# Five small moves of work around the turn of a fused linear-attention and gated-MLP forward and backward kernel: key sums, stores of r, loads of x, the r sums of tile 6, a fill between squares

## The chip, the core and the metric

The kernel runs on one core of a Trainium2 chip. All times are microseconds of device time of that core (us); one execution is one run of the whole program. Six runs of the kernel before took 828.26 to 830.65, median 829.41.

## What is computed

The reference is one transformer block and its gradients. With `x` of 2048 rows and 640 columns in bf16, 32 heads of 20 columns each, and `g` the gradient of the output:

```python
pq, pk = phi(q), phi(k)                    # phi(t) = where(t > 0, t + 1, exp(t)) + 1e-6
kv  = einsum("bhsd,bhse->bhde", pk, v)
z   = einsum("bhsd->bhd", pk)              # the key sums
den = einsum("bhqd,bhd->bhq", pq, z)[..., None] + 1e-6
o   = einsum("bhqd,bhde->bhqe", pq, kv) / den
h   = x + o.reshape(B, S, D) @ wo          # q, k, v = layernorm(x) @ wqkv
out = h + (silu(n @ w1) * (n @ w3)) @ w2   # n = layernorm(h)
```

The outputs are `out` and the gradients of `x`, `wqkv`, `wo`, `w1`, `w3`, `w2`.

## The kernel before

The 2048 rows are 16 tiles (`ST`) of 128 rows, in four groups (`SC`) of four; 640 columns are five blocks (`DT`) of 128. The order of the work on every engine is written out by hand: an engine executes its instructions in the order in which the Python code issues them, and the framework adds the waits that data and reused buffers ask for. So is the order in the three DMA queues that matter here: SP's (`dma`, `dmaT`, the second a transposing DMA), GpSimd's (`dmaG`) and ScalarE's (`A.dma_start`). An instruction that waits at the head of an engine or a queue holds up all behind it.

**Phase 1** (lines 430 to 570) normalises x, makes keys, values and a part of the queries, and sums over the keys. `m_part` accumulates a key-by-x matrix for each column block, `z_late` the key sums of blocks 2 to 4. `z_row` (line 324) spreads the key sums over all partitions: it multiplies a matrix of ones by diagonal matrices `dz` (two for blocks 0 and 1, three for blocks 2 to 4) into PSUM, and ScalarE copies the result to `Zb`. It is called twice (lines 533, 534), on the two banks of one PSUM tile `bigx`. The queries then get their denominators: for tile t, `r_prod` multiplies pq by `Zb` on GpSimd into `pr`, `r_red` sums per head on VectorE, `r_inv` adds 1e-6 and inverts, `r_scale` scales pq to r in place, and `r_T` issues a transposing DMA of it into `pqT` on SP's queue. `r_head` is `r_red`, `r_inv`, `r_scale` and `r_T` in one.

**The turn** is the single call of `run` at lines 801 to 809, a list of steps. `q_late` makes the remaining queries (each two halves of five 320-column matmuls, line 260); `f2_wT(i)` makes a row block of the folded output matrix and transposes it by DMA into `Wp` (line 628), five DMAs in all; `f2_half(t, j)` (line 780, body from 578) makes half j of h for tile t: five matmuls of `pqT` with `Wp` (line 586) into a PSUM tile `at`, then either an addition of x on VectorE (line 591; it is so for the j = 0 halves of tiles 0 to 3 and for tile 4) or, with x added on TensorE by the identity (line 584), a copy on ScalarE (line 589), and then statistics on VectorE. The second half ends with mean and variance, and GpSimd raises the variance to the power -1/2 (`ln_rs`, line 154). `f2_hn(t)` normalises the row tile on VectorE (line 160) and stores it on SP's queue; `f2_ht(t)` transposes it on TensorE (tile `trh`, line 677) and ScalarE copies it to `pqT` (line 678). `mlp_ghh(n)` is five 512-column matmuls of a piece of the MLP's gradient, which depend on nothing that the turn makes; ScalarE copies the result. `r_store`, `r4_out`, `q_out`, `f2_m_out`, `f2_w_out` are stores on GpSimd's queue. `load_x` brings x back into `x_sb` on SP's queue.

Two pools of buffers matter. `pql`, with four buffers, holds pq, later r, of tiles 4 to 7 and afterwards of the tiles that `r_load` brings back. The tag `h2`, with two buffers, holds the products `pr` of even tiles, then `hn` of tiles 2 and 3.

**The MLP** (line 849 on) goes through four groups of 512 rows and 14 column blocks each. `mlp(c, fc)` issues ten 512-column matmuls (line 369; five, from w1, then five, from w3), and ScalarE reads their PSUM tiles four times: `sig`, `s2`, `gate` (lines 705 to 707) and `up` (line 713). The PSUM tag `mm` has four buffers; TensorE gets one back when ScalarE has read it. The buffers of `up` lie on memory that the turn used for `pr` of tile 7. For each two blocks VectorE computes seven products and sums (line 741), and GpSimd's queue stores two of them to `gg_d`; the buffers of `gate` are two, so that block pair k + 2 may be written only when pair k's store has landed.

**Behind the MLP** come the weight gradients of w2 (line 955), the gradient towards h (line 1000) and the attention's backward part. In the squares (lines 1252 to 1295) five blocks of `dwoT` and five of `gm` are made: `square` (six matmuls of 140 columns into a PSUM tile of tag `dkv`, three buffers), `unload` (ScalarE copies 380 columns, then VectorE 260, line 1236), and for `gm` a few transposes `trk` into another `dkv` buffer (line 1284) with a copy on VectorE (line 1285). `fill(1)` puts eight 320-column matmuls of an independent job (line 1198) between them. Five `tensor_scalar` of VectorE make `gzd` (line 1278).

Of the kernel before, what the change touches and what calls it, by code (L numbers as in the profile page):

```python
# [55 lines left out]
def kernel(  # L56
# [19 lines left out]
    V, A, T, G, SY = nc.vector, nc.scalar, nc.tensor, nc.gpsimd, nc.sync  # L76
# [51 lines left out]
    Zb = cp.tile([P, D], BF16, name="Zb")  # L128

    class Stats:  # L130
# [8 lines left out]
        def run(self, src, a, b):  # L139
            for t in range(a, b):  # L140
                for j in range(2):
                    self.part(src, t, j)
# [32 lines left out]
    pf = pool("pf", "right")  # L175
    p1 = pool("p1", "right")
    ps = pool("p1p", space=PSUM)
# [6 lines left out]
    def load_x(a, b):  # L184
        dma(out=x_sb[:, a:b, :], in_=xS[:, a:b, :])
# [77 lines left out]
    def p1_mm(t, n0):  # L263
        acc = ps.tile([P, 2, 512], F32, name="big", bufs=2)
        for j in range(2):
            p1_half(acc[:, j, 0:HD], t, n0 + j * HD)
        return acc
# [40 lines left out]
    dz = {}  # L308
# [12 lines left out]
        for m in ms:  # L321
            z_diag(m)

    def z_row(ms, acc):

        for i, m in enumerate(ms):
            T.matmul(acc[:, i * P:(i + 1) * P], lhsT=ones[:], rhs=dz[m][:], start=(i == 0), stop=True,
                     skip_group_check=True)
        A.copy(out=Zb[:, ms[0] * P:(ms[-1] + 1) * P], in_=acc[:, 0:len(ms) * P])

    pr = {}

# [145 lines left out]
    for t in range(ST):  # L478
        k = p1_mm(t, D)
# [49 lines left out]
        go()  # L529
    z_late((2, 3, 4), big())  # L530
    m_part(2, range(10))
    zr = ps.tile([P, 2, 512], F32, name="bigx", tag="big", bufs=2)
    z_row((0, 1), zr[:, 0])
    z_row((2, 3, 4), zr[:, 1])
    r_prod(0)
    q_tile(5)
    r_prod(1)
# [31 lines left out]
    m_part(4, range(11, ST))  # L569
    m_end(4)  # L570
    ps.release()
    load_x(0, 2)


    ps = pool("pap", space=PSUM)
    hn, hnT, hhT = {}, {}, {}
# [43 lines left out]
    def f2_wT(i):  # L620

        acc = [ps.tile([P, 512], F32, name="wt", tag=("o2", "at")[i % 2], bufs=2) for _ in range(2)]
        for c, a, b, bank, off, first in SQ:
            T.matmul(acc[bank][:, off:off + (b - a) * DH], lhsT=wo[:, c, i * P:(i + 1) * P],
                     rhs=bd[:, c, a * DH:b * DH], start=first, stop=True, skip_group_check=True)
        for bank, (a, b) in enumerate(((0, SPLIT_D), (SPLIT_D, H))):
            (A.copy, V.tensor_copy)[bank](out=pkx[0][:, i, a * DH:b * DH], in_=acc[bank][:, 0:(b - a) * DH])
        dmaT(out=Wp[:, :, i * P:(i + 1) * P], in_=pkx[0][:, i, :])
# [30 lines left out]
        dma(out=pqs[t], in_=pq_v[:, t, :])  # L659

    def f2_hn(t):
        hn[t] = (pf.tile([P, D], BF16, name="hn", tag="h2", bufs=2) if 2 <= t < TPC else
                 pf.tile([P, D], BF16, name="hn", bufs=2))
        ln2.norm(hn[t][:], x_sb[:, t, :], t)
        dma(out=hn_v[:, t, :], in_=hn[t][:])
# [131 lines left out]
    def kv3():  # L797
        for m in (2, 3, 4):
            f2_kv(m)

    run((q_late, 10, f2_mT), (q_late, 11, kv3), (phi_rest,), (r_store, 4, 5),
        (q_late, 12, lambda: (f2_wT(0), f2_wT(1))), (q_late, 13, lambda: (f2_wT(2), f2_wT(3))), (phi_rest,),
        (q_late, 14, lambda: f2_wT(4)), (load_x, 2, 4), (r_head, 5), (r_prod, 7), (r_red, 6), (r_inv, 6), (f2_m_out,), (f2_w_out,),
        (load_x, 4, 8), (q_out, 10, 14), (r_store, 5, 6), (load_w2T, 8 * P, 10 * P), (mlp_ghh, 4), (q_late, 15),
        (sig_table,), (f2_half, 0, 0), (f2_half, 1, 0), (mlp_ghh, 5), (f2_half, 0, 1), (f2_half, 1, 1), (f2_hn, 0),
        (f2_half, 2, 0), (f2_hn, 1), (load_w2T, 10 * P, F), (f2_half, 2, 1),
        (f2_ht, 0), (f2_half, 3, 0), (f2_hn, 2), (f2_half, 3, 1), (mlp_ghh, 6), (f2_ht, 1), (mlp_ghh, 7), (f2_ht, 2),
        (f2_hn, 3), (f2_half, 4, 0), (f2_ht, 3), (f2_half, 4, 1), (r_scale, 6), (r_T, 6), (r_red, 7), (r_inv, 7),
        (r_scale, 7), (r_T, 7), (r4_out,), (r_store, 6, 8), (q_out, 8, 10))
    p1.release()  # L810
    pa = pool("pa", "right")

# [36 lines left out]
    for c in range(SC):  # L849
# [8 lines left out]
        for fc in range(FT):  # L858
# [22 lines left out]
            if c == SC - 1 and fc in (1, 2, 5, 6):  # L881
                i = (1, 2, 5, 6).index(fc)
# [29 lines left out]
    ps = pool("pcp", space=PSUM)  # L912
# [35 lines left out]
    for fc in range(FT - 1):  # L948
        b, i = divmod(fc, 4)
        if fc == FT - 2:  # L950
            gw2_tail()
        acc = ps.tile([P, 2, 512], F32, name="gw", bufs=4)
        for j in range(2):
            for t in range(ST):
                T.matmul(acc[:, j, 0:HD], lhsT=hb[b][:, t, i * P:(i + 1) * P], rhs=g2[:, t, j * HD:(j + 1) * HD],  # L955
                         start=(t == 0), stop=(t == ST - 1))
# [23 lines left out]
    ps = pool("pbp", space=PSUM)  # L980
# [3 lines left out]
    gz = cp.tile([P, DT], F32, name="gz")  # L984
# [234 lines left out]
    ps = pool("pdp", space=PSUM)  # L1219
# [14 lines left out]
    def unload(acc, out):  # L1234
        for bank, (a, b) in enumerate(((0, SPLIT_D), (SPLIT_D, H))):
            (A.copy, V.tensor_copy)[bank](out=out[:, a * DH:b * DH], in_=acc[:, bank, 0:(b - a) * DH])

    def fill(n):
        for _ in range(n):
            next(jobs, None)  # L1240
# [4 lines left out]
    for m, (a, b) in enumerate(M_H):  # L1245
        n = (b - a) * DH
        acc = ps.tile([P, 512], F32, name="gkvT", tag="dkv", bufs=3)
        for c in range(DT):
            T.matmul(acc[:, 0:n], lhsT=woT[:, c, m * P:(m + 1) * P], rhs=QT[:, c, a * DH:b * DH], start=(c == 0),
                     stop=(c == DT - 1))  # L1250
        masked(gkvT, acc[:, 0:n], m)
    dwoT = U1.tile([P, DT, D], BF16, name="dwoT", tag="W6")
    for i in range(DT):
        unload(square(qp, kvN, i), dwoT[:, i, :])
        if i > 0:
            fill(1)
    br.release()
    bo.release()
# [4 lines left out]
    gzd = small[:, 3 * DT, :].rearrange("p (m q) -> p m q", q=P)  # L1263
# [5 lines left out]
    def load_pk(c):  # L1269
        pkb[c] = dx.tile([P, 2, D], BF16, name="pkb", bufs=4)  # L1270
        (dma if c < 4 else dmaG)(out=pkb[c][:], in_=pk_v[:, c * 2:(c + 1) * 2, :])
# [2 lines left out]
    g_k = gqkv[1] = U1.tile([P, ST, D], BF16, name="g_k", tag="S0")  # L1274
    for n in range(4):
        load_pk(n)
    for m in range(DT):
        V.tensor_scalar(out=gzd[:, m, :], in0=ident[:], scalar1=gz[:, m:m + 1], scalar2=None, op0=ALU.mult)

    for i, (c, ms) in enumerate(SQ_BLOCKS):  # L1280
        unload(square(wqT[:, 2 * DT:, :], gkvT, i), gm[:, i, :])
        tr = ps.tile([P, len(ms), P], BF16, name="trk", tag="dkv", bufs=3)
        for k, m in enumerate(ms):
            T.transpose(tr[:, k, :], gkvT[:, m, c * P:(c + 1) * P], ident[:])
        V.tensor_copy(out=gkv_b[:, c, ms[0] * P:(ms[-1] + 1) * P].rearrange("p (i q) -> p i q", q=P), in_=tr[:])
        if i > 0:
            fill(1)
        dmaT(out=wqT[:, 2 * DT:, i * P:(i + 1) * P], in_=gm[:, i, :])
    acc = d_acc()
    for m in range(DT):  # L1290
        T.matmul(acc[:, m // 4, m % 4 * P:(m % 4 + 1) * P], lhsT=ones[:], rhs=gzd[:, m, :], start=(m % 4 == 0),
                 stop=True, skip_group_check=True)
# [3 lines left out]
    for t in range(ST):  # L1296
        c, i = divmod(t, TPC)
        u = t // 2
        acc = d_acc()
        for j in range(2):  # L1300
            for k in range(DT):
                T.matmul(acc[:, j, 0:HD], lhsT=xnT[c][:, k, i * P:(i + 1) * P], rhs=gm[:, k, j * HD:(j + 1) * HD],  # L1302
                         start=(k == 0), stop=(k == DT - 1))
# [7 lines left out]
        if t in (2, 5, 8, 11, 14):  # L1311
            n = t // 3
            acc = square(mN, gkv_b, n)
            k = (4, 0, 1, 2, 3)[n]
# [48 lines left out]
    ps = pool("pep", space=PSUM)  # L1363
# [24 lines left out]
    ps = pool("pfp", space=PSUM)  # L1388
# [45 lines left out]
```

## Time and profile before

| what | value |
|---|---|
| median of six runs | 829.41 us |
| the profiled execution's own time | 829.01 us |
| its span in the trace | 827.3 us |
| TensorE matmuls (PE) busy | 816.4 us, 99% of the span |
| VectorE (DVE) busy | 453.6 us, 55% |
| ScalarE (ACT) busy | 319.1 us, 39% |
| GpSimd (POOL) busy | 135.1 us, 16% |
| DMA, all queues | 157.59 MB, mean 190 GB/s |
| granted TensorE clock | 1.00 in every stretch looked at |

The profile is of one execution; times within it count from the start of its span. The profiled execution took 829.01, 1.7 more than its span and 0.4 less than the median of the six. A line of the timeline reads: start, duration, engine, line of the code, operation, output from inputs, shape, how many are merged; in brackets the time for which the engine stood idle before it, and the engine, tile and line that ended this. SPq and POOLq are the DMA queues.

### The profile page before, as it was taken

The page shows a single profiled execution, that of the slowest core. Times are in us where ns is not written, and L with a number is a line of the kernel's source. Part 1 is how long each engine was busy: PE and PEld are TensorE (multiplying, and loading weights), DVE is VectorE, ACT ScalarE, POOL GpSimd, SP SyncE. Part 2 cuts the span into 40 slices and gives each one's busy share as a digit, 9 for nine tenths or more (in the row PEclk, how much of TensorE's full clock was granted, in tenths as well). Part 3 has the DMA queues.
Part 4 walks back from the last instruction along what each step waited for, and adds up shares of the span by engine and source line. Part 5 has one row for each costly group of instructions (what it writes and reads, how often), then busy time and mean ns, then how long its engine had stood idle before and what let it go on. Part 6 is the DMA issues. An engine that isn't in the chain of part 4 may idle for free.

```text
span 827.3 us, 14189 instructions
## 1 busy us (share of the span) xinstructions
PE 816.4 (99%) x5523; PEld 523.5 (63%) x5551; DVE 453.6 (55%) x960; ACT 319.1 (39%) x609; POOL 135.1 (16%) x196
## 2 busy tenths in 40 slices
PE   8999999999999999999999999999999999999998
PEld 5677644555555555777777777777777777555554
DVE  7859798899898566400057777772681545200000
ACT  5855777665655666011121222222212333211111
POOL 2334343233222212100001111110220000000000
PEclk9999999999999999999999999999999999999999
DMA  9899999696594465999978999358995788985781
GB/s 258 209 313 200 199 284 288 217 221 170 133 211 134 143 206 161 205 245 232 267 168 181 186 217 202 61 106 174 259 222 100 163 191 172 215 193 141 161 172 38
DMA packets 318355, 157.59 MB, mean 190 GB/s; under 512 B 235472, under 2 KB 311472, under 8 KB 318288
## 3 DMA queue, kind: packets, MB, share of 16 engines
q1 hardware_dynamic: 286272, 120.65, 63.8%
q0 software_dynamic: 7376, 24.81, 9.0%
q10 hardware_dynamic: 24640, 11.23, 7.6%
q8 instruction: 43, 0.70, 0.3%
q14 instruction: 24, 0.20, 0.1%
HBM read 48.15 MB, written 51.46 MB: 120 GB/s over the span
## 4 chain that ended last, share of the span: by engine, by line
PE 93%; DMA 3%; DVE 1%; ACT 1%; SPq 1%; issue 1%; ACTq 0%; DVEq 0%; POOLq 0%
PE job L1198 19%; PE mm L369 18%; PE ghn L1000 14%; PE gxn L1356 8%; PE o L766 7%; PE gw L955 7%; PE big L260 3%; PE gwo L1085 3%; PE gr L1057 3%; PE dkv L1302 3%; PE macc L400 3%; PE at L586 2%; DMA x_sb<-in_A_x_dram 1%; DMA g2T<-in_grad_out_dram 1%; PE dkv L1230 1%
## 5 line engine op out<-in xcount | busy, mean ns | idle before, releaser
L1198 PE MATMUL job<-gb,hnN 128*128 128x432 bf16 (+2 forms) x656 | 117.0, 342 | 0.0
L1000 PEld LDWEIGHTS <-ggb 128*128 128x128 bf16 x864 | 84.5, 98 | 32.8
L1198 PEld LDWEIGHTS <-hnN 128*128 128x128 bf16 x656 | 63.6, 98 | 53.4
L369 PE MATMUL mm<-pqT,w 128*128 128x512 bf16 x396 | 93.2, 379 | 1.1 <-ACT up L713 0.4
L369 PEld LDWEIGHTS <-w 128*128 128x128 bf16 x540 | 52.5, 98 | 64.1 <-issue 2.2
L1202 ACT CAST obs<-job 128x432 bf16<-128x432 f32 (+3 forms) x61 | 29.4, 481 | 123.0 <-PE job L1198 123.0
L766 PE MATMUL o<-w,hhT 128*128 128x320 bf16 x448 | 67.5, 299 | 0.1
L1000 PE MATMUL ghn<-w13a,ggb 128*128 128x320 bf16 x448 | 63.5, 299 | 0.0
L1000 PE MATMUL ghn<-w13b,ggb 128*128 128x320 bf16 x416 | 61.4, 299 | 0.0
L369 PE MATMUL mm<-g2T,w2T 128*128 128x512 bf16 x227 | 58.8, 379 | 1.2 <-ACT gate L707 0.5
L766 PEld LDWEIGHTS <-hhT 128*128 128x128 bf16 x448 | 43.8, 98 | 23.6
L955 PE MATMUL gw<-g,hb 128*128 128x320 bf16 x416 | 56.8, 299 | 0.0
L1065 POOL TENSOR_TENSOR sz<-Zb,g_h 128x640 f32<-128x640 bf16 x16 | 20.2, 1262 | 199.3 <-DVE g_h L1063 199.3
L955 PEld LDWEIGHTS <-hb 128*128 128x128 bf16 x416 | 40.6, 98 | 16.0 <-issue 0.3
L1356 PE MATMUL gxn<-wqT,gT 128*128 128x320 bf16 x320 | 48.7, 299 | 0.0
L389 ACT CAST ghh<-mm 128x512 bf16<-128x512 f32 x48 | 28.3, 589 | 43.9 <-PE mm L369 38.4
L705 ACT ACTIVATE sig<-mm 128x512 bf16<-128x512 f32 x56 | 33.7, 603 | 25.8 <-PE mm L369 24.1
L1012 ACT ACTIVATE gs<-ghn 128x640 bf16<-128x640 f32 x16 | 11.3, 704 | 79.0 <-PE ghn L1000 69.1
L369 PEld LDWEIGHTS <-w2T 128*128 128x128 bf16 x260 | 25.3, 98 | 25.3 <-issue 2.1
L260 PE MATMUL big<-wqkv,pqT 128*128 128x320 bf16 x260 | 39.3, 299 | 1.3 <-DMA wqkv<-in_A_wqkv_dram 0.6
L260 PEld LDWEIGHTS <-pqT 128*128 128x128 bf16 x320 | 30.5, 98 | 14.2 <-ACT pqT L256 2.0
L1356 PEld LDWEIGHTS <-gT 128*128 128x128 bf16 x320 | 31.3, 98 | 12.2
(201 smaller groups left out, 1285.0 us busy)
## 6 DMA issues: line engine op xcount, KB each, us to landing
hh_d<-hhT SPq DMA_DIRECT2D x24, 256.0 KB, 2.7
gg_d<-gate POOLq DMA_DIRECT2D x24, 256.0 KB, 4.3
gg_d<-ghh POOLq DMA_DIRECT2D x24, 256.0 KB, 3.5
ggb<-gg_d SPq DMA_DIRECT2D x6, 896.0 KB, 5.8
ggb<-gg_d SPq DMA_DIRECT2D x6, 832.0 KB, 8.5
out_dram<-obs ACTq DMA_DIRECT2D x39, 108.0 KB, 3.2
x_sb<-in_A_x_dram SPq DMA_DIRECT2D x6, 640.0 KB, 7.4
ggb<-gg_d SPq DMA_DIRECT2D x2, 1728.0 KB, 13.2
```

What stands on the lines that cost most here:

```text
L260: T.matmul(acc, lhsT=pqT[:, c, t * P:(t + 1) * P], rhs=wqkv[:, c, n0:n0 + HD], start=(c == 0), stop=(c == DT - 1))
L369: T.matmul(acc[:], lhsT=w[:, c, fc * P:(fc + 1) * P], rhs=rhs[:, c, :], start=(c == 0), stop=(c == DT - 1))
L389: A.copy(out=ghh[n // 2][:, n % 2, :], in_=acc[:])
L400: T.matmul(macc[m][j][:, 0:n], lhsT=pk_all[:, t, m * P:(m + 1) * P], rhs=x_ext[:, t, j * HD:j * HD + n], start=(t == 0), stop=(t == ST - 1))
L705: A.activation(sig[:, i, :], gp[:], AF.Sigmoid)
L766: T.matmul(o2["ps"][:, 0:HD], lhsT=hhT[c][:, fc, i * P:(i + 1) * P], rhs=w2[:, fc, j * HD:(j + 1) * HD], start=(fc == 0), stop=(fc == FT - 1))
L955: T.matmul(acc[:, j, 0:HD], lhsT=hb[b][:, t, i * P:(i + 1) * P], rhs=g2[:, t, j * HD:(j + 1) * HD], start=(t == 0), stop=(t == ST - 1))
L1000: T.matmul(acc[:, j, 0:HD], lhsT=ggb[t // 2][:, k, lo:lo + P], rhs=rhs[:, j * HD:(j + 1) * HD], start=(k == 0), stop=(k == NG - 1))
L1057: T.matmul(gr[t][:, j, 0:HD], lhsT=ghT[t][:, c, :], rhs=wT2[:, c, j * HD:(j + 1) * HD], start=(c == 0), stop=(c == DT - 1))
L1198: T.matmul(acc[:, 0:n], lhsT=lhs[:, t, m * P:(m + 1) * P], rhs=rhs(t), start=(t == 0), stop=(t == ST - 1))
L1202: A.copy(out=ob, in_=acc[:, 0:n])
L1356: T.matmul(acc[:, j, 0:HD], lhsT=g, rhs=wqT[:, k, j * HD:(j + 1) * HD], start=(k == 0), stop=(k == 14))
```

## The change

Five things change; what is computed stays the same.

- `z_row` becomes `z_rows`: the five matmuls for both banks are issued first, then the two copies.
- In the turn, `r4_out` (the store of r of tiles 0 to 3) goes from the end of the list to behind `r_store` of tile 4. `q_out` of tiles 8 and 9 goes from the end to ahead of `q_out` of tiles 10 to 13, and `r_store` of tile 5 ahead of `f2_m_out`, `f2_w_out`, `q_out`.
- x is loaded in two pieces of four tiles: tiles 0 to 3 where tiles 0 and 1 were, and tiles 4 to 7 right behind `f2_wT(4)`, where tiles 2 and 3 were, ahead of `r_T` of tile 5.
- `r_red` and `r_inv` of tile 6 go from ahead of `f2_half(0, 0)` to behind `f2_hn(3)`; `r_scale` and `r_T` of tile 6 follow them there, ahead of the additions of tile 4. As `pr` of tile 6 then lives longer, `hn` of tiles 2 and 3 takes buffers of `pql` (those of tiles 4 and 5) in place of `h2`. The three `mlp_ghh` 5, 6 and 7 each come one or two steps later, and `f2_hn(3)` ahead of `f2_ht(2)`.
- In the squares, the fill behind block 1 of `dwoT` goes to behind block 0 of `gm`, and `gzd` is made there too, behind the first two copies.

```diff
-    def z_row(ms, acc):
-        for i, m in enumerate(ms):
-            T.matmul(acc[:, i * P:(i + 1) * P], lhsT=ones[:], rhs=dz[m][:], start=(i == 0), stop=True,
-                     skip_group_check=True)
-        A.copy(out=Zb[:, ms[0] * P:(ms[-1] + 1) * P], in_=acc[:, 0:len(ms) * P])
+    def z_rows(parts, acc):
+        for k, ms in enumerate(parts):
+            for i, m in enumerate(ms):
+                T.matmul(acc[:, k, i * P:(i + 1) * P], lhsT=ones[:], rhs=dz[m][:], start=(i == 0), stop=True,
+                         skip_group_check=True)
+        for k, ms in enumerate(parts):
+            A.copy(out=Zb[:, ms[0] * P:(ms[-1] + 1) * P], in_=acc[:, k, 0:len(ms) * P])
...
-    z_row((0, 1), zr[:, 0])
-    z_row((2, 3, 4), zr[:, 1])
+    z_rows(((0, 1), (2, 3, 4)), ps.tile([P, 2, 512], F32, name="bigx", tag="big", bufs=2))
...
-    load_x(0, 2)
+    load_x(0, 4)
...
-        hn[t] = (pf.tile([P, D], BF16, name="hn", tag="h2", bufs=2) if 2 <= t < TPC else
+        hn[t] = (pf.tile([P, D], BF16, name="hn", tag="pql", bufs=4) if 2 <= t < TPC else
...
-    run((q_late, 10, f2_mT), (q_late, 11, kv3), (phi_rest,), (r_store, 4, 5),
+    run((q_late, 10, f2_mT), (q_late, 11, kv3), (phi_rest,), (r_store, 4, 5), (r4_out,),
         (q_late, 12, lambda: (f2_wT(0), f2_wT(1))), (q_late, 13, lambda: (f2_wT(2), f2_wT(3))), (phi_rest,),
-        (q_late, 14, lambda: f2_wT(4)), (load_x, 2, 4), (r_head, 5), (r_prod, 7), (r_red, 6), (r_inv, 6), (f2_m_out,), (f2_w_out,),
-        (load_x, 4, 8), (q_out, 10, 14), (r_store, 5, 6), (load_w2T, 8 * P, 10 * P), (mlp_ghh, 4), (q_late, 15),
-        (sig_table,), (f2_half, 0, 0), (f2_half, 1, 0), (mlp_ghh, 5), (f2_half, 0, 1), (f2_half, 1, 1), (f2_hn, 0),
-        (f2_half, 2, 0), (f2_hn, 1), (load_w2T, 10 * P, F), (f2_half, 2, 1),
-        (f2_ht, 0), (f2_half, 3, 0), (f2_hn, 2), (f2_half, 3, 1), (mlp_ghh, 6), (f2_ht, 1), (mlp_ghh, 7), (f2_ht, 2),
-        (f2_hn, 3), (f2_half, 4, 0), (f2_ht, 3), (f2_half, 4, 1), (r_scale, 6), (r_T, 6), (r_red, 7), (r_inv, 7),
-        (r_scale, 7), (r_T, 7), (r4_out,), (r_store, 6, 8), (q_out, 8, 10))
+        (q_late, 14, lambda: f2_wT(4)), (load_x, 4, 8), (r_head, 5), (r_prod, 7), (r_store, 5, 6), (f2_m_out,),
+        (f2_w_out,), (q_out, 8, 10), (q_out, 10, 14), (load_w2T, 8 * P, 10 * P), (mlp_ghh, 4), (q_late, 15),
+        (sig_table,), (f2_half, 0, 0), (f2_half, 1, 0), (f2_half, 0, 1), (f2_half, 1, 1), (f2_hn, 0), (mlp_ghh, 5),
+        (f2_half, 2, 0), (f2_hn, 1), (load_w2T, 10 * P, F), (f2_half, 2, 1), (f2_ht, 0), (f2_half, 3, 0), (f2_hn, 2),
+        (f2_half, 3, 1), (f2_ht, 1), (mlp_ghh, 6), (f2_hn, 3), (f2_ht, 2), (r_red, 6), (r_inv, 6), (r_scale, 6), (r_T, 6),
+        (f2_half, 4, 0), (f2_ht, 3), (mlp_ghh, 7), (f2_half, 4, 1), (r_red, 7), (r_inv, 7), (r_scale, 7), (r_T, 7),
+        (r_store, 6, 8))
...
         unload(square(qp, kvN, i), dwoT[:, i, :])
-        if i > 0:
+        if i > 1:
             fill(1)
...
-    for m in range(DT):
-        V.tensor_scalar(out=gzd[:, m, :], in0=ident[:], scalar1=gz[:, m:m + 1], scalar2=None, op0=ALU.mult)
...
         V.tensor_copy(out=gkv_b[:, c, ms[0] * P:(ms[-1] + 1) * P].rearrange("p (i q) -> p i q", q=P), in_=tr[:])
-        if i > 0:
-            fill(1)
+        fill(1)
+        if i == 0:
+            for m in range(DT):
+                V.tensor_scalar(out=gzd[:, m, :], in0=ident[:], scalar1=gz[:, m:m + 1], scalar2=None, op0=ALU.mult)
         dmaT(out=wqT[:, 2 * DT:, i * P:(i + 1) * P], in_=gm[:, i, :])
```

## Prediction

> **What bounds the kernel now.** I read first the busy time per engine, then the busy time in stretches, then each engine's timeline where TensorE (PE) is not full. The page says that the kernel is PE's:
>
> ```profile
> PE 816.4 (99%) x5523; PEld 523.5 (63%) x5551; DVE 453.6 (55%) x960; ACT 319.1 (39%) x609; POOL 135.1 (16%) x196
> ```
>
> So no step can win more than PE's holes. The stretches (window, its length, PE busy first) show where they are:
>
> ```profile
> 57.00:59.00 2.00, 1.54 (x15) 1.10 (x13) 0.00 (x0) 0.70 (x2) 0.00 (x0) 1.00 1.07 385
> 94.00:101.50 7.50, 6.99 (x55) 4.27 (x54) 5.14 (x16) 4.60 (x8) 1.97 (x4) 1.00 1.13 215
> 101.50:118.00 16.50, 15.32 (x73) 7.22 (x74) 14.31 (x30) 10.94 (x23) 6.58 (x9) 1.00 1.06 286
> ...
> 328.00:580.00 252.00, 252.00 (x1902) 181.57 (x1901) 118.16 (x230) 47.35 (x81) 24.81 (x24) 1.00 0.88 187
> 580.00:583.00 3.00, 2.37 (x28) 1.90 (x27) 2.32 (x10) 1.25 (x3) 0.54 (x1) 1.00 0.78 218
> ```
>
> From 118 on PE waits for nobody but at 580 and at the very end (between 118 and 328 some single matmul records are missing), so a lead that PE has at 118 lasts to the end. "Busy" counts a matmul's modelled tail, so I take a hole from start to start: a step is 0.055 for a 128-column matmul, 0.136 for 320 columns (ten in 1.36), 0.216 for 512 (fifteen in 3.24).
>
> The key sums, in the timeline:
>
> ```profile
> 57.58 0.27 PE L327 MATMUL bigx<-dz,ones 128*128 128x128 bf16 x2
> 57.89 0.37 ACT L329 CAST Zb<-bigx 128x256 bf16<-128x256 f32 x1 [2.64 <-PE bigx L327]
> 58.31 0.33 PE L327 MATMUL bigx<-dz,ones 128*128 128x128 bf16 x3 [0.46 <-ACT Zb L329]
> ```
>
> The third matmul was due at 57.58 + 2 x 0.055 = 57.69 and came at 58.31: 0.62 lost to the first copy. The turn, PE's own lines:
>
> ```profile
> 94.78 0.45 PE L677 MATMUL trh<-ident,hn 128*128 128x128 bf16 x5 [0.35 <-DVE hn L160]
> ...
> 107.25 1.24 PE L369 MATMUL mm<-pqT,w 128*128 128x512 bf16 x5 [0.36 <-ACT up L713]
> 108.72 2.32 PE L369 MATMUL mm<-pqT,w 128*128 128x512 bf16 x10 [0.23 <-ACT gate L707]
> ...
> 117.47 1.24 PE L369 MATMUL mm<-g2T,w2T 128*128 128x512 bf16 x5 [0.49 <-ACT gate L707]
> ```
>
> Start to start these are 0.52 (hn of tile 0), 0.51 and 0.39 (ScalarE late with `up` and `gate`), 0.65; before 101.3 two more, 0.14 at the transposes of hn 3 and 0.27 at the MLP's first matmul. Behind them stand ScalarE and VectorE:
>
> ```profile
> 106.61 0.59 ACT L713 CAST up<-mm 128x512 bf16<-128x512 f32 x1 [2.44 <-POOL ln_rs L154]
> ...
> 116.83 0.59 ACT L707 CAST gate<-mm 128x512 bf16<-128x512 f32 x1 [1.62 <-DMA gg_d<-gate]
> ```
>
> ```profile
> 103.00 0.49 DVE L591 TENSOR_TENSOR x_sb<-at,x_sb 128x320 bf16<-128x320 f32 x1 [2.96 <-DMA x_sb<-in_A_x_dram]
> ...
> 106.02 0.87 DVE L348 TENSOR_REDUCE rden<-pr 128x16 f32<-128x320 f32 x2
> ```
>
> `up` lies on `pr` of tile 7. It starts right behind the first of the two sums at 106.02, so I read that sum as the releaser (the line names GpSimd, done at 106.51). VectorE got there late because it stood 2.96 for x of tiles 4 to 7. The squares:
>
> ```profile
> 580.80 0.88 ACT L1236 CAST small<-dkv 128x380 bf16<-128x380 f32 x2
> 581.31 0.43 DVE L1236 CAST small<-dkv 128x260 bf16<-128x260 f32 x1 [0.22 <-ACT small L1236]
> 581.79 0.33 PE L1284 MATMUL trk<-ident,bd 128*128 128x128 bf16 x3 [0.63 <-DVE small L1236]
> ```
>
> The second group of transposes waits until block 0 is copied out; six steps of 0.06 after 580.67 it was due at 581.00, so 0.79 is lost.
>
> **The change part by part**, in before's clock.
>
> Key sums: the five matmuls follow each other, PE gains **0.62**. Both copies now wait for the fifth, but the second starts at about 58.45 for 58.68, so GpSimd's products and the full VectorE queue behind them gain only 0.23.
>
> Wp: five transposing DMAs are issued back to back from 82.5 to 87.8, 1.2 each, each 2.6 to landing, so the last lands at 90.45; it starts from VectorE's queue and moves only by 0.23, to 90.2. PE needs it at `f2_half(0, 1)`. Before, `mlp_ghh(5)` (5 x 0.216 = 1.08) stood in front and PE came at 91.14; now PE comes at 90.06 - 0.62 = 89.44 and waits to 90.3. That eats the 0.62 and a little more: PE has tile 0's transposes in reach at 94.4 (due at 94.26 before). But hn 0 is there: VectorE no longer does tile 6's sums (89.44 to 90.83, 1.39) ahead of the first addition, and hn 0 comes at 93.3, bound by GpSimd, whose queue of stores (now with 0.79 for tiles 8 and 9 in it) ends at 92.7. So the 0.52 goes: PE does the transposes at 94.4 for 94.78.
>
> To the MLP: PE then has 0.28 + 0.68 + 0.82 + 0.28 + 1.08 + 0.28 + 0.68 = 4.1, to 98.5, and waits for hn 3. VectorE had it at 99.60 to 100.05; with statistics some 0.9 earlier I put it at 98.7 to 99.1. PE loses 0.65 there, then does 0.28 + 1.08 + 0.68 and starts the MLP at 101.2, for 101.34: hardly a gain yet.
>
> In the MLP: VectorE does tile 6 (0.86 + 0.9 + 0.9, to 101.7), then the additions of tile 4 without the 2.96 (x asked for at 89 and not 92.8), and reaches the sum of tile 7 at 103.8, so `up` starts at 104.3 for 106.61. ScalarE is ready for it only at 104.0. The 0.51 and 0.39 go: six groups of 1.08 from 101.2 end at 107.7, for 108.72. **Lead 1.05.** Block pair 0 is stored some 1.8 earlier, and 960 KB of stores (r of tiles 0 to 3, pq of 8 and 9) are out of its way, so the 1.62 of `gate` and PE's 0.65 go too (bounds 0 to 0.65; I take 0.65, as the landing moves by more than PE). **Lead 1.70.**
>
> Squares: the 1.09 of the fill now lies between block 0 and the second transposes; 0.11 + 1.09 + 0.33 = 1.53 against 1.07 that the copies take. `gzd` (0.90 of VectorE) comes behind block 0's copies, and block 1's have 1.6. At `dwoT`, block 2 follows at once; its buffer is free at 574.73 and it is due at 574.89. Gain **0.79** (bounds 0.4 to 0.79).
>
> Costed at nothing: `r4_out` at 78.7 in GpSimd's queue, idle to 87.3; its 640 KB and 320 KB more of x go where the DMA engines were 0.60 busy at 130 GB/s (80 to 90). If they delay the last Wp, PE pays one for one (0 to 1.0; I take 0, since the last Wp comes at the end of that stretch). `r_load` of tiles 8 and 9 now waits for r of tiles 6 and 7 to have left their buffers; r of tile 6 goes at 101.7 and 104.9, and SP comes to that load at 114.2, so some 9 hide it. On SP's queue x of tiles 4 to 7 goes ahead of `r_T(5)` (0.4 to 1.6 of issue, by the three loads of x in the turn). On GpSimd's queue r of tile 5 waits for VectorE's scaling, at 88.9, and four more stores wait behind it; that is in the 92.7 above. The three `mlp_ghh` cost PE what they did.
>
> Sum: 1.70 + 0.79 = 2.49 off the profiled execution's 829.01 gives 826.5; off the median of 829.41, which I forecast, **826.9**. All holes together (0.62 + 2.48 + 0.79) allow 3.9.
>
> **What I can't price: the landing of r_T of tile 5.** hn 3 now takes tile 5's `pql` buffer and waits until that transpose has landed. Before, nobody waited for it:
>
> ```profile
> L359 SPq DMA_TRANSPOSE pqT<-pql x1: 2736/2736/2736, 90.0 to 90.0; - x1
> ...
> DMA to landing us min/median/max: 11.2/11.2/11.2
> ```
>
> That is 101.2, too late for 98.7. The same DMA for tile 4 took 3.7 with few stores about; from 89.5 that is 93.2. Now 640 KB of x stand ahead of it and not 320, and 320 KB more of stores beside it; at the 215 GB/s of 94 to 101.5 this adds 3.0: 104.2. Ends 93.2 and 104.2. I take 98 to 99: the stores (819 KB of W) now reach the DMA engines about a microsecond after it, and the tile's own store goes first.
>
> The Trainium skill, "DMA: Bandwidth & Descriptors", section on queues, rings and completion order, says that a DMA's count lands only after all earlier writes of that DMA engine, of other queues too. The trace agrees: W, pq and r stores landed at 99 to 101.4, as the transpose did (89.4 + 9.6, 90.2 + 10.7 and 91.0 + 10.3 against 90.0 + 11.2). It speaks against the change: by this rule, as an estimate, the count waits for the stores in flight, to 99 to 101, and 0.3 to 2.3 of the gain goes; by the row of tile 4 nothing goes.
>
> **Rivals.** (B) The transpose lands as late as before, 101.2: hn 3 is 2.5 late, PE loses the 2.5 one for one, and the squares and the rest only make up for it: **829.4**. For it: the 11.2. Against: `r_T` of tiles 6 and 7 landed in 3.5 and 5.5 beside a store of 640 KB. (C) Slower: it lands at 104.2, 5.5 late, **832.4**; this decides from 102.9 on. (D) The turn's lead is lost behind it, as VectorE is busy 48.26 of 50 from 150 to 200; only the squares stay, **828.6**. Against: VectorE leads by as much as PE there.
>
> **Numbers.** Forecast (landing up to 99.5, 826.0 to 827.7) 0.55; B (99.5 to 102.9) 0.27; C 0.10; D 0.08. About 0.2%, 1.66, is what a measurement of this kernel can tell from no change. Faster is the forecast and a little of D, 0.57; slower C and a little of D, 0.11; within, 0.32. The range goes from 826.0 (the forecast with 0.9 more of the 3.9) to 829.9; it leaves out C and the part of B that lands behind 101.7, about 0.08. The forecast alone is 826.0 to 827.7.
>
> **What would show it.** No bracket at the key sums and at `trk`; `up` at ScalarE without a long wait; VectorE without the 2.96; PE at 118 some 1.7 ahead. Wrong, if VectorE's hn of tile 3 (line 160) waits for a DMA, PE then stands before the fourth `trh`, and the MLP starts later than 101.3.

## The result and the profile after

Over all executions the median fell from 829.05 us (78 executions, 826.5 to 833.6) to **827.13 us** (39 executions, 825.9 to 834.0). The ratio is 0.9979, 95% interval 0.9971 to 0.9986: 1.7 us faster, between 1.2 and 2.4. The forecast was 2.5 us faster: 826.9 from a median of 829.41. In the three later series of executions the kernel before had medians of 828.40, 827.77 and 828.31, so the size of the gain depends in part on which executions of it are taken. The spread shrank too: eight of ten executions lay between 827.3 and 830.6 before and lie between 826.1 and 828.2 now.

The page's busy times of the changed kernel, and its busy time in the stretches that were shown of before (window, its length, busy time and count of PE, PEld, DVE, ACT and POOL, granted clock, DMA share, GB/s):

```profile
PE 815.9 (99%) x5524; PEld 522.9 (63%) x5551; DVE 454.1 (55%) x960; ACT 319.0 (39%) x609; POOL 134.1 (16%) x196
```

```profile
57.00:59.00 2.00, 2.00 (x19) 1.50 (x18) 0.00 (x0) 0.75 (x2) 0.04 (x1) 1.00 1.06 380
94.00:101.50 7.50, 6.63 (x54) 4.22 (x54) 6.53 (x19) 4.08 (x8) 1.51 (x3) 1.00 1.10 316
101.50:118.00 16.50, 16.39 (x82) 8.04 (x83) 15.60 (x33) 13.73 (x28) 5.32 (x8) 1.00 0.96 237
580.00:583.00 3.00, 3.00 (x35) 2.43 (x34) 2.13 (x9) 1.21 (x4) 0.54 (x1) 1.00 0.97 307
```

PE is full at the key sums (2.00 for 1.54), almost full through the MLP's first groups (16.39 for 15.32) and full at the squares (3.00 for 2.37). In the turn it is less busy than before (6.63 for 6.99). Where it waits, its timeline tells:

```profile
57.64 0.44 PE L328 MATMUL bigx<-dz,ones 128*128 128x128 bf16 x5
...
78.87 1.11 PE L421 MATMUL kv<-mT,wqkv 128*128 128x160 bf16 x15 [0.55 <-DMA mT<-mbs]
...
90.55 0.85 PE L586 MATMUL at<-Wp,pqT 128*128 128x320 bf16 x5 [0.22 <-DMA Wp<-pkx]
...
99.76 0.45 PE L677 MATMUL trh<-ident,hn 128*128 128x128 bf16 x5 [0.81 <-DVE hn L160]
...
101.81 8.80 PE L371 MATMUL mm<-pqT,w 128*128 128x512 bf16 x39
...
116.39 1.24 PE L371 MATMUL mm<-g2T,w2T 128*128 128x512 bf16 x5
```

The five key sums run in one piece. But at 78.87 there is a bracket that before didn't have: the `kv` matmuls (line 421, before 419) wait for the fourth transposed `mT`, and they start where they started before (78.90). From start to start this hole is 0.71, where before it was 0.18, too little for a bracket. Then 0.38 goes at Wp and 0.98 at the fourth `trh`. Behind that the MLP runs without a bracket, and the ninth group of the gate half starts at 116.39 for 117.47: PE leads by 1.08, not by 1.70. VectorE and ScalarE (timeline, both engines):

```profile
101.87 0.48 DVE L591 TENSOR_TENSOR x_sb<-at,x_sb 128x320 bf16<-128x320 f32 x1
...
104.74 0.58 ACT L713 CAST up<-mm 128x512 bf16<-128x512 f32 x1
...
114.65 0.59 ACT L707 CAST gate<-mm 128x512 bf16<-128x512 f32 x1
```

None of the three has a bracket; before they had 2.96 for x, 2.44 for `up`, 1.62 for `gate`. At the squares the second transposes come 0.33 after the start of their square (580.59), without a bracket:

```profile
580.92 0.33 PE L1282 MATMUL trk<-ident,bd 128*128 128x128 bf16 x3
```

The transpose of r of tile 5, which couldn't be priced (its instructions and its landing):

```profile
L361 SPq DMA_TRANSPOSE pqT<-pql x1: 1297/1297/1297, 90.0 to 90.0; - x1
...
DMA to landing us min/median/max: 7.2/7.2/7.2
```

It landed at 97.1, earlier than the 98 to 99 that the forecast took, and nobody waited for it.

The two profiled executions differ by only 0.87 in PE's last start (823.83 and 822.96), though the turn gave 1.08 and the squares 0.79. The missing 1.0 lies between 116 and 551: 0.2 ahead of 398, and two waits of 0.36 and 0.46 for `ghT` (line 1057, at 503 and 521). Those waits are the subject of one question below.

### The profile page after: what moved, and what is told of

Its sections match the earlier page's. It is cut to its first block, busy times and chain, and to the rows that moved or that the text cites. A ratio compares the mean times of both kernels' runs of the same rounds, so it can differ in the third digit from the quotient of the medians.

```text
span 826.5 us, 14190 instructions
## 1 busy us (share of the span) xinstructions
PE 815.9 (99%) x5524; PEld 522.9 (63%) x5551; DVE 454.1 (55%) x960; ACT 319.0 (39%) x609; POOL 134.1 (16%) x196
## 4 chain that ended last, share of the span: by engine, by line
PE 89%; DVE 4%; DMA 4%; ACT 1%; issue 1%; POOL 1%; SPq 0%; ACTq 0%; DVEq 0%
PE mm L371 20%; PE job L1198 19%; PE ghn L1000 11%; PE gxn L1356 8%; PE o L766 7%; PE gw L955 7%; PE gwo L1085 3%; PE dkv L1302 3%; PE big L260 2%; PE macc L402 2%; PE gr L1057 2%; DMA ghT<-g_h 2%; PE at L586 2%; DVE st L147 1%; DMA x_sb<-in_A_x_dram 1%
## 5 line engine op out<-in xcount | busy, mean ns | idle before, releaser
L1012 ACT ACTIVATE gs<-ghn 128x640 bf16<-128x640 f32 x16 | 11.2, 703 | 79.8 <-PE ghn L1000 79.8
```

## The experiments

Three marks on PE cut an execution into stretches that can be compared across kernels, however the start of an execution went: the first key sum, the first `kv` of the last block (near 78), the first matmul of the MLP, and the ninth group of the gate half (near 116). One profiled execution each, us from start to start (r5_behind and w2T_late_swap are told in their own parts):

| kernel | key sum to kv | kv to MLP | MLP to ninth group | the last two together |
|---|---|---|---|---|
| before | 21.32 | 22.44 | 16.13 | 38.57 |
| before_2 | 21.14 | 22.44 | 14.60 | 37.04 |
| sq_only | 21.14 | 22.44 | 16.46 | 38.90 |
| z_only | 21.09 | 22.44 | 16.43 | 38.87 |
| turn_only | 21.57 | 22.96 | 14.58 | 37.54 |
| after | 21.23 | 22.94 | 14.58 | 37.52 |
| after_2 | 20.52 | 22.94 | 14.58 | 37.52 |
| red6_ahead | 20.52 | 23.25 | 14.58 | 37.83 |
| r4_end | 20.52 | 22.94 | 14.72 | 37.66 |
| x_late | 21.24 | 22.96 | 15.56 | 38.52 |
| ghh7_ahead | 20.70 | 22.44 | 14.58 | 37.02 |
| ghh7_2 | 20.70 | 22.44 | 14.58 | 37.02 |

### z_only: the key sums alone

```diff
-    z_row((0, 1), zr[:, 0])
-    z_row((2, 3, 4), zr[:, 1])
+    z_rows(((0, 1), (2, 3, 4)), ps.tile([P, 2, 512], F32, name="bigx", tag="big", bufs=2))
```

> Before with the key sums alone as in the change. Theory (the 0.62 us that PE wins at 57.7 is lost again at kv, line 421, where PE has to wait for the fourth mT to land at 78.8): within 0.2 us of before; the profile shows no wait at the key sums, and at kv a loss from start to start of 0.6 to 0.8 us (0.18 before), and from 80 on every row at the time of before. Rival (the 0.62 is carried to the end): 0.6 us faster, kv at 78.3.

Measured: ratio 0.9998, interval 0.9986 to 1.0011. PE's `kv` line in its timeline:

```profile
78.62 1.11 PE L421 MATMUL kv<-mT,wqkv 128*128 128x160 bf16 x15 [0.41 <-DMA mT<-mbs]
```

The theory stands for this execution: the hole moved from the key sums to `kv` (0.58 from start to start), and `kv` comes 21.09 after the first key sum, as without the edit (21.14). But it isn't the whole truth. In after_2, red6_ahead and r4_end, which hold the same edit, `kv` comes after 20.52, without a wait: 0.62 sooner to the hundredth. There `mT` landed 4.9 to 5.1 after it was asked for (at 72.3 and 72.5; at 75.0 in r4_end, whose execution started 2.2 later), ahead of PE. So the key sums are worth 0 to 0.62, as the landing of `mT` falls: nothing in z_only, after and x_late, all of it in three, 0.44 in the two ghh7 kernels.

### sq_only: the squares alone

```diff
-        if i > 0:
-            fill(1)
+        fill(1)
+        if i == 0:
+            for m in range(DT):
+                V.tensor_scalar(out=gzd[:, m, :], in0=ident[:], scalar1=gz[:, m:m + 1], scalar2=None, op0=ALU.mult)
```

> Before with the squares alone as in the change (two fills, gzd behind block 0). Theory and rival alike: 0.8 us faster, as PE waits for nothing after 580. If a wait comes instead elsewhere (dwoT, where a fill is gone), 0.4 us or less. If the two waits for ghT at line 1057 that the changed kernel's profile shows come from the squares, they cannot show here before 571, so they should be absent.

Measured: ratio 0.9992, interval 0.9980 to 1.0004, so the time alone doesn't settle 0.8 us. The profile does: from the last `gr` matmul (line 1057) to the last `trk` it is 35.57 in before, before_2, z_only and turn_only, and 34.78 to 34.79 in sq_only, after and after_2. That is 0.78 to 0.79 each time, and nothing is lost at `dwoT`. A wait for `ghT` of 0.16 is here at 521, where none of this kernel's edits has acted yet.

### turn_only: the change without key sums and squares

```diff
+    z_row((0, 1), zr[:, 0])
+    z_row((2, 3, 4), zr[:, 1])
-    z_rows(((0, 1), (2, 3, 4)), ps.tile([P, 2, 512], F32, name="bigx", tag="big", bufs=2))
```

(and the lines of the squares as before)

> The change without the key sums and without the squares. Theory (the turn alone makes the lead of 1.1 us at 118): 1.1 us faster than before, 0.8 us slower than the change; the MLP's first matmul at 101.8, the ninth gate-half at 116.4, kv at 78.9 with a loss below 0.3. Rival (the lead of 1.1 is the key sums' 0.62 and only 0.5 of the turn): 0.5 us faster than before, MLP from 102.3.

Measured: ratio 0.9999, interval 0.9990 to 1.0009. **This missed**: no 1.1 us in the time. In the profile the turn does what the theory said, 37.54 against 38.57 of the first profile of before. But `kv` lost 0.43, not below 0.3: it waited for an `mT` asked for at 72.6, before any edit of this run acts, so that from the first key sum to the ninth group the execution takes 59.11, against 59.89 of before. Both hold together only if other executions of before do not take 38.57; before_2 was run for that.

### before_2: the kernel before once more

> The kernel before, a second time, for the spread of one execution: ratio 1.000, from the first key sum to the ninth group of the gate half 59.7 to 60.1 us (59.89 and, with the squares changed, 60.04 so far), 0.79 lost at the squares, and waits for ghT of 0 to 0.8 in all.

Measured: ratio 1.0003, interval 0.9992 to 1.0014, but the profile broke the expectation: 58.18 from the first key sum to the ninth group, not 59.7 to 60.1. This execution has none of the losses at `up`, `gate` and the ninth group. Its timeline (SP's issues, VectorE's addition of tile 4, ScalarE's `up` and PE's MLP):

```profile
89.47 1.44 SPq L359 DMA_TRANSPOSE pqT<-pql  x1
90.97 1.46 SPq L185 DMA_DIRECT2D x_sb<-in_A_x_dram  x1
...
100.94 0.49 DVE L591 TENSOR_TENSOR x_sb<-at,x_sb 128x320 bf16<-128x320 f32 x1 [1.41 <-DMA x_sb<-in_A_x_dram]
...
104.55 0.58 ACT L713 CAST up<-mm 128x512 bf16<-128x512 f32 x1 [0.89 <-POOL ln_rs L154]
...
115.42 1.24 PE L369 MATMUL mm<-g2T,w2T 128*128 128x512 bf16 x5
```

The same rows of SP in the first profile of before, then SP and VectorE in z_only, which has before's turn too:

```profile
92.79 1.56 SPq L185 DMA_DIRECT2D x_sb<-in_A_x_dram  x1
```

```profile
89.71 1.37 SPq L361 DMA_TRANSPOSE pqT<-pql  x1
91.14 1.51 SPq L185 DMA_DIRECT2D x_sb<-in_A_x_dram  x1
...
102.89 0.49 DVE L591 TENSOR_TENSOR x_sb<-at,x_sb 128x320 bf16<-128x320 f32 x1 [3.12 <-DMA x_sb<-in_A_x_dram]
```

The mechanism is the one that the forecast read, seen from its good side: it hangs on the landing of x of tiles 4 to 7. In the first profile x landed at 102.9, here at 100.9; as this whole turn runs 0.5 earlier, x is 1.5 sooner within it. `up` still waits 0.89 on ScalarE, but PE waits for nothing. Why x landed sooner is open. It isn't the issue of `r_T(5)` ahead of it on SP's queue (2.74 in the first profile, 1.44 here): z_only issued it in 1.37 and asked for x at 91.1, yet x landed only at 102.8 and VectorE stood 3.12 for it. In before_2 the stores beside x were faster too: that of W landed in 8.0 and not 9.6, that of pq in 9.1 and not 10.7. So the kernel before has two kinds of executions, 38.6 to 38.9 (three profiles) and 37.0 (one), and the turn of the change takes 37.5 in all three profiles that have it whole (turn_only, after, after_2): shorter than the first kind and 0.5 longer than the second.

### x_late: x loaded as before

```diff
-    load_x(0, 4)
+    load_x(0, 2)
...
-(load_x, 4, 8), (r_head, 5), (r_prod, 7), ...
+(load_x, 2, 4), (r_head, 5), (r_prod, 7), ...
-(q_out, 8, 10), (q_out, 10, 14), ...
+(load_x, 4, 8), (q_out, 8, 10), (q_out, 10, 14), ...
```

> The change with x loaded as before (tiles 2 and 3 in the turn, tiles 4 to 7 behind the transpose of r of tile 5, issued near 92). Theory (x for tiles 4 to 7 then lands at 100 or later, the addition of tile 4 waits in VectorE's queue ahead of the sums of tile 7, and up and gate come late again): VectorE's addition at 102 waits for x up to 1 us or more, up waits again, 0.5 to 1.1 us slower than the change. Rival (x is there in time with the changed order of the norms, since the addition comes only at 101.9): no difference from the change.

Measured: ratio 0.9985 to before, interval 0.9975 to 0.9996, too wide to be told from the change. The profiled execution loses 0.98 between the MLP's start and the ninth group (15.56 for 14.58), and its timeline names the chain, VectorE, ScalarE, PE:

```profile
103.21 0.49 DVE L591 TENSOR_TENSOR x_sb<-at,x_sb 128x320 bf16<-128x320 f32 x1 [1.55 <-DMA x_sb<-in_A_x_dram]
...
116.44 0.59 ACT L707 CAST gate<-mm 128x512 bf16<-128x512 f32 x1 [1.77 <-DMA gg_d<-gate]
...
117.08 1.24 PE L371 MATMUL mm<-g2T,w2T 128*128 128x512 bf16 x5 [0.84 <-ACT gate L707]
```

The theory stands, the rival falls: the addition waits 1.55 for x, everything behind it on VectorE and ScalarE comes that much later, the store of `gate` goes at 111.8 for 110.5, ScalarE waits 1.77 until it has landed and the buffer is free, and PE pays 1.0: most of it, 0.8, before the ninth group, where `gate` waits for `gg_d`, and 0.2 at 108.2. The early load of x is the part of the turn that earns.

### r4_end: r of tiles 0 to 3 stored at the end

```diff
-(phi_rest,), (r_store, 4, 5), (r4_out,),
+(phi_rest,), (r_store, 4, 5),
...
-        (r_store, 6, 8))
+        (r4_out,), (r_store, 6, 8))
```

> The change with the store of r of tiles 0 to 3 (640 KB) put back to the end of the turn, ahead of the store of r of tiles 6 and 7, as before. Theory (that store stood ahead of the store of gate, gg_d, on GpSimd's queue and in the DMA engines; out of the way it is worth the wait of gate at 116): gate waits again for the landing of gg_d at the fifth block, and PE loses 0.4 to 0.9 before the ninth group of the gate half; 0.4 to 0.9 us slower than the change. Rival (x loaded sooner makes up and gate early enough by itself): gg_d lands before gate wants it, no difference. Either way kv and Wp stand as in the change, since nothing of the store is in flight at 79 to 84; if Wp lands earlier by over 0.2, the early store had a price there.

Measured: ratio 0.9984, interval 0.9973 to 0.9995, not to be told from the change. In the profile the store of `gate` lands in 5.3 instead of 4.0, ScalarE's `gate` waits 1.13 for it, and PE loses 0.14 (14.72 for 14.58):

```profile
117.34 0.59 ACT L707 CAST gate<-mm 128x512 bf16<-128x512 f32 x1 [1.13 <-DMA gg_d<-gate]
...
117.98 1.24 PE L371 MATMUL mm<-g2T,w2T 128*128 128x512 bf16 x5 [0.19 <-ACT gate L707]
```

The direction is the theory's, the size is below it. Wp is waited for as long as in the change (0.36 and 0.38), so the early store costs nothing at 79 to 84.

### red6_ahead: the sums of tile 6 ahead of the norms

```diff
-(r_prod, 7), (r_store, 5, 6), (f2_m_out,),
+(r_prod, 7), (r_red, 6), (r_inv, 6), (r_store, 5, 6), (f2_m_out,),
...
-(f2_ht, 2), (r_red, 6), (r_inv, 6), (r_scale, 6), (r_T, 6),
+(f2_ht, 2), (r_scale, 6), (r_T, 6),
```

> The change with the sums of r of tile 6 and their inverse (0.87 + 0.18 + 0.35 of VectorE) put back ahead of the first additions and norms. Theory (hn of tile 0 is then late by up to 0.9 and PE waits at the first trh as before, while hn of tile 3 comes 0.0 to 0.3 later; what counts is the start of the MLP, which waits for hn of tile 3): PE loses 0.4 to 0.5 at the first trh, but of it most is taken out of the 0.98 before the fourth trh, so the MLP starts at 101.8 to 102.2 and the kernel is 0 to 0.4 us slower than the change. Rival (the prediction's account: hn of tile 3 moves with VectorE's whole queue): 0.9 later, MLP at 102.7, 0.9 us slower.

Measured: ratio 0.9989, interval 0.9980 to 0.9997. From `kv` to the MLP it takes 23.25 for 22.94, 0.31 more, inside the theory's 0 to 0.4 and far from the rival's 0.9. The detail was wrong: no wait at the first `trh`; 0.15 of the loss lies at Wp (0.53 for 0.38) and 0.16 at the third `trh`.

### r5_behind: the store of r of tile 5 behind the big stores

```diff
-(r_prod, 7), (r_store, 5, 6), (f2_m_out,), (f2_w_out,), (q_out, 8, 10), (q_out, 10, 14),
+(r_prod, 7), (f2_m_out,), (f2_w_out,), (q_out, 8, 10), (q_out, 10, 14), (r_store, 5, 6),
```

> The change with the store of r of tile 5 put back behind the stores of m, W and pq of tiles 8 to 13 on GpSimd's queue, as before, so that these 1.8 MB are in flight when the transpose of r of tile 5 is issued at 90. Theory (the transpose lands late beside those stores, and hn of tile 3 then waits for it): landing at 99 to 101.2 instead of 97.1; where it lands behind 98.9, hn of tile 3 (line 160) waits for a DMA and the MLP starts later by the same amount, up to 2.3 us, so up to 2.3 us slower than the change. Rival (the order on GpSimd's queue is without effect on that landing): landing at 97, no difference from the change.

Measured: 832.52 us, ratio to before 1.0053, interval 1.0041 to 1.0065; with the change at 0.9979 that makes 6 us between two places for one store. The transpose of r of tile 5 with its landing, then VectorE and PE, then the busy time ahead of the hole and behind it:

```profile
L361 SPq DMA_TRANSPOSE pqT<-pql x1: 1333/1333/1333, 90.2 to 90.2; - x1
...
DMA to landing us min/median/max: 12.6/12.6/12.6
```

```profile
102.94 0.45 DVE L160 TENSOR_SCALAR hn<-x_sb,ln_mv,ln_rs 128x640 bf16<-128x640 bf16 x1 [4.45 <-DMA pqT<-pql]
...
103.45 0.71 PE L677 MATMUL trh<-ident,hn 128*128 128x128 bf16 x5 [4.39 <-DVE hn L160]
103.95 2.34 PE L371 MATMUL mm<-g2T,w2T 128*128 128x512 bf16 x5
```

```profile
95.00:99.00 4.00, 3.95 (x35) 2.60 (x33) 3.33 (x11) 2.90 (x6) 0.97 (x2) 1.00 1.09 283
103.40:107.00 3.60, 3.55 (x15) 1.87 (x16) 3.04 (x7) 1.28 (x2) 0.00 (x0) 0.54 1.15 320
```

The theory stands in its direction and was too mild in its size: the landing came at 102.8, not by 101.2, and PE paid twice. It waited 4.56 at the fourth `trh` for 0.98, and then the granted clock (the last column but two) stood at 0.54 for 3.6 us: five 512-column matmuls took 2.34 for 1.24. From the first key sum to the MLP this makes 49.16 for 44.17, 5.0 more: 3.6 of wait and 1.6 of slow clock (3.63 from the fourth `trh` to the MLP, for 2.05), less 0.2 that PE waited less at Wp and at the third `trh`. All five executions of this kernel took 831.6 to 833.7, with a mean granted clock of 0.996 to 0.998; 34 of the 39 of the change have 1.000.

### w2T_late_swap: mT asked for sooner

This is ghh7_ahead (next) with one more edit:

```diff
     r_head(0)
-    load_w2T(4 * P, 8 * P)
...
     r_head(3)
+    load_w2T(4 * P, 8 * P)
```

> The version with the last group of the gate half ahead of the transposes of hn of tile 3, and besides the load of w2T of blocks 4 to 7 moved on SP's queue from behind r of tile 0 to behind r of tile 3, so that the fourth transpose of m, which holds kv up, is issued some 3 us earlier. Theory (kv waits for that landing, and what was won at the key sums is lost there): no wait at kv, kv at 78.1 to 78.2; the wait for Wp behind it grows by what kv wins, unless Wp moves with kv; 0 to 0.4 us faster than that version. Rival (the later load of w2T falls on the loads of x and Wp and delays them): Wp lands later than 90.5, up to 0.5 us slower.

Measured: 832.03 us, ratio 1.0045, interval 1.0025 to 1.0065. Half the theory held: `kv` comes at 78.21, 20.53 after the first key sum, and waits for nothing. The rival took the rest, at ten times its price:

```profile
90.85 2.83 PE L586 MATMUL at<-Wp,pqT 128*128 128x320 bf16 x10 [2.68 <-DMA Wp<-pkx]
```

The transposing load now stands at 75.9 on SP's queue, takes 5.0 to issue and 9.4 to land, and the five transposes of Wp behind it land in 5.1 (median) for 2.7. PE waits twice (2.7 and 1.1), and behind the first wait ten 320-column matmuls take 2.83 for 1.52: the clock is half again (0.56 in 91 to 94). So this load, at least, can't be moved into 76 to 88 on SP's queue for free.

### ghh7_ahead and ghh7_2: a group ahead of the fourth trh

```diff
-        (f2_half, 4, 0), (f2_ht, 3), (mlp_ghh, 7), (f2_half, 4, 1), ...
+        (f2_half, 4, 0), (mlp_ghh, 7), (f2_ht, 3), (f2_half, 4, 1), ...
```

> The change with the last group of the MLP's gate half (mlp_ghh 7, 1.08 us of PE) moved ahead of the transposes of hn of tile 3, where PE waits 0.98 us in the changed kernel. Theory (that wait is the whole of what keeps the MLP's start at 101.8): the group fills the wait, the MLP starts at 100.9 and the kernel is 0.8 to 1.0 us faster than the change, if VectorE and ScalarE keep up. Rival (ScalarE and VectorE set the end of the MLP's first groups, so that the lead is lost behind 101.8 at up or gate): within 0.2 us of the change, with new waits for up or gate between 102 and 109.

> The version with the last group of the gate half ahead of the transposes of hn of tile 3, beside the changed kernel on one chip. Theory: PE's 0.98 before the fourth trh falls to about 0.5 before the MLP's first matmul and 0.5 to 0.6 us are won, if kv stands at the same time in both; 0.3 to 1.0 faster than the change. Rival (the gain of the first look, 1.03 from the first key sum to the ninth group, was kv's luck, which had 0.54 of it): 0.0 to 0.3 faster.

Measured: ratios to before 0.9978 (0.9968 to 0.9987) and 0.9975 (0.9965 to 0.9986), medians 826.53 and 826.00. PE in ghh7_2:

```profile
98.90 0.44 PE L677 MATMUL trh<-ident,hn 128*128 128x128 bf16 x5
...
100.33 2.97 PE L371 MATMUL mm<-pqT,w 128*128 128x512 bf16 x13 [0.31 <-ACT pqT L678]
```

The group of 1.08 lies where PE stood, and 0.47 of the hole is left, now at the MLP's first matmul, where ScalarE copies the last transposes out. From `kv` to the MLP it is 22.44 for 22.94 in both: 0.50 won, as the theory of ghh7_2 has it; the 1.03 that ghh7_ahead won from the first key sum to the ninth group held 0.53 of `kv`'s luck, as its rival says. Neither the 0.8 to 1.0 that was expected of ghh7_ahead nor its rival's new waits for `up` and `gate` came. Beside the change in one series the medians are 826.00 and 827.25. It is the fastest version here, and from the first key sum to the ninth group it takes 57.72, where the change took 58.75 and 58.04 and before 59.89 and 58.18, though its interval against before overlaps with the change's.

It undoes a part of the change. Counted in PE's steps, the change moves `mlp_ghh` 5 by two, 6 by one and 7 by three, not each by one or two: `mlp_ghh` 7 went from ahead of the third `trh` to behind the fourth, and so left the wait for hn of tile 3 unfilled.

### after_2: the changed kernel once more

> The changed kernel as it is, a second time. If the two waits of PE for ghT (line 1057, 0.36 and 0.46 us at 503 and 521) are a matter of one execution, they are absent or elsewhere here, and the profiled execution is some 0.8 us shorter than the first, if its kv does not wait more; if the change causes them, they are here again. Counted from the first key sum to the ninth group of the gate half it takes 58.2 to 58.9 us (58.75 in the first profile, 59.89 before): 58.2 if kv doesn't wait for the fourth transpose of m, 58.9 if it waits as in the first.

Measured: median 827.25 against 828.31 of before; the ratio came out at 1.0005 with an interval of 0.9977 to 1.0032, since three of its executions took 830 to 837, with a mean granted clock of 0.993 to 0.998. The profile took 58.04 from the first key sum to the ninth group, a little below the 58.2 expected without a wait at `kv`, and PE's last start was 1.39 sooner than in the first profile. PE and the first issue of Wp's transposes on SP's queue:

```profile
77.74 1.12 PE L421 MATMUL kv<-mT,wqkv 128*128 128x160 bf16 x15
...
81.45 6.66 SPq L628 DMA_TRANSPOSE Wp<-pkx  x5
...
89.56 0.85 PE L586 MATMUL at<-Wp,pqT 128*128 128x320 bf16 x5 [0.28 <-DMA Wp<-pkx]
...
100.68 8.80 PE L371 MATMUL mm<-pqT,w 128*128 128x512 bf16 x39
```

Here the 0.62 of the key sums reaches the MLP: the first key sum to the MLP takes 43.46, for 44.17 in the first profile. The two waits for `ghT` are gone; one of 0.2 stands at 484, and `gate` has one of 0.55 at 150. z_only had such a wait at `gate` (0.71 at 145), r4_end 0.3 for `ghT`, sq_only 0.16. So they come and go from execution to execution, and without the turn too. Whether the change makes them likelier isn't settled by fourteen profiles.

## Why the prediction was right in direction and 0.8 us too large

**Key sums, +0.62 (the term that was mis-sized).** At their place the 0.62 was won in every execution. The step that failed is that PE would bring it to Wp. The forecast had `kv` at 78.28; it came at 78.87, since `mT` landed at 78.8. The trace of before held the warning: there `mT` was asked for at 73.0 with 5.9 to landing, 78.9, and `kv`, due at 78.72, came at 78.90 without a bracket:

```profile
72.96 2.10 SPq L412 DMA_TRANSPOSE mT<-mbs  x1
...
77.36 1.52 PE L260 MATMUL mm<-wqkv,pqT 128*128 128x320 bf16 x10
78.90 1.11 PE L419 MATMUL kv<-mT,wqkv 128*128 128x160 bf16 x15
```

A wait that has only just begun shows no bracket. In the profiled execution of the change the term measured 0; over the table it is 0 to 0.62.

**Wp, said to move by only 0.23 and to eat the 0.62.** By that account a late `kv` would have cost nothing, since PE waits for Wp either way. But Wp doesn't stand still: its first transpose is issued 3.64 to 3.71 behind `kv` in every profile but w2T_late_swap's, whether `kv` is early or late (82.52 behind 78.87 in after, 81.45 behind 77.74 in after_2). So the 0.6 that `kv` came late went through to the MLP, and where `kv` was on time so did the gain.

**From kv to the MLP.** The forecast's own numbers make 22.92 (101.2 less 78.28); measured 22.94 in after and after_2. That the sum agrees is in part luck, as the parts differed: Wp cost 0.38 where 0.9 was foreseen, the fourth `trh` 0.98 where it was 0.65. Against before this stretch is 0.50 longer, which "hardly a gain yet" hid, and ghh7_2 shows that the 0.50 lay in the order of two entries.

**In the MLP, lead 1.05 and then 1.70.** The forecast's 14.57 (115.77 less 101.2) is 14.58 in the trace. x landed at 94.2, the waits of 2.96, 2.44 and 1.62 are gone, and so is PE's 0.65. x_late shows that the early x does it (0.98), r4_end that the early store of r adds 0.14. The lead of 1.70 came out as 1.08 only because all of it sat on a `kv` 0.6 late.

**Squares, 0.79.** 0.78 to 0.79, in every profile with the edit.

**r_T of tile 5, taken at 98 to 99.** 97.1, and 96.1 to 97.0 in turn_only, after_2, red6_ahead and the two ghh7 kernels. The stores' rows agree with the reason given: the 800 KB of W go out at 90.9 and land at 99.0, behind it. The Trainium skill, "DMA: Bandwidth & Descriptors", section on queues, rings and completion order, has a count land only after earlier writes of that engine. r5_behind is compatible with that but doesn't show it: stores issued from 89.6 on landed at 99.8 to 102.6 and the transpose at 102.8, yet of these only W was issued ahead of the transpose (90.2). Whether the rule or the traffic beside it holds the transpose up stays open. The forecast's estimate from the rule, 99 to 101, counted such stores as earlier; the row 97.1 decides. Rivals B and C didn't happen in the change, but r5_behind shows that they named the right wait at the right place, at too low a price: the landing came 3.6 after hn of tile 3 starts in the change (99.26), PE's hole grew by these 3.6, one for one, and the fallen clock added 1.6: 5.0 in all, with the 0.2 won ahead of it.

**Rival D** (the turn's lead lost behind it) didn't happen in the stretch to 148; the chance waits at `gate` and `ghT` are of its kind and took 1.0 from the profiled execution.

**The base.** The sum was made against one execution, and the 1.55 at `up`, `gate` and the ninth group is not in every execution of before. Averaged over the profiles, `kv` to ninth group went from 38.35 (four of before's turn) to 37.53 (turn_only, after, after_2): 0.82. With 0.78 of the squares and 0 to 0.62 of the key sums that makes 1.6 to 2.2, where the times say 1.7 (1.2 to 2.4). That turn_only showed nothing in its series is told by the same mixture only in part: its median of 828.3 lies inside before's 826.8 to 830.7, where before's two kinds of executions lie on either side of it. Its interval, 0.9990 to 1.0009, just allows the 0.82; the time alone doesn't show that the turn gains.

## What to carry to other kernels

Before a lead is carried down an engine, look at each later instruction that another engine or a DMA feeds and compare its start with that feeder's landing: where they agree within a tenth, the lead ends there, bracket or not. A hole that hangs on a landing should be read in several executions before it is priced, since here one execution in four had none of it. And a store moved by 2 us past others, with a transposing DMA beside it, can cost more than a whole change wins (6 us against 1.7), so the order of a queue's stores deserves an experiment of its own.

## What the runs showed of the hardware

A hole of 4.4 us on PE (r5_behind) halved the granted clock afterwards, and so did one of 2.7 (w2T_late_swap) and one of 1.9 at 13 us in r4_end, from which the later start of that execution comes. The busy time of the three slow stretches, in this order (the granted clock is the last column but two):

```profile
103.31:106.72 3.41, 3.27 (x13) 1.67 (x14) 3.12 (x8) 1.08 (x2) 0.00 (x0) 0.50 1.19 330
90.21:93.62 3.41, 2.77 (x11) 1.46 (x11) 0.99 (x2) 0.27 (x2) 2.43 (x4) 0.50 1.06 244
15.71:19.12 3.41, 3.41 (x16) 2.00 (x15) 3.13 (x11) 1.23 (x2) 1.13 (x2) 0.50 0.98 338
```

Each lasted 3.41 us. A hole of 1.6 (at 13 us in r5_behind) and those of 1.2 and less left the clock at 1.00. The Trainium skill, "TensorE: Matmul & The Clock Gate", part 1, gives an idle window of about 3.4 us, after which the clock halves, and as long to come back. The length of the slow stretches agrees, but the second and third hole show that less idle time than such a window can be enough. So a late DMA costs its lateness and, in these runs from between 1.6 and 1.9 us on, the slow stretch too: 1.6 us in r5_behind, and 1.3 over the ten matmuls of w2T_late_swap.

The transposing DMA of r of tile 5 took from 6.2 to 12.6 us to land over these orders of the stores, and its issue differed with nothing changed: 2.74 and 1.44 us of SP's queue in two executions of before, with 11.2 and 9.7 to landing. Whether x came in time hung on its own landing, which in before's turn took 9.9 to 11.7 and did not follow that issue.
